# Block 0 of an attention kernel: output rows gathered in chunks of seven whole heads, the last four heads used where they are turned

## The chip, the cores and the metric

The kernel runs on one core of one Trainium2 chip. The metric is the device time of one execution in microseconds (us), lower is better. PE is the tensor engine, DVE the vector engine, ACT the scalar engine, POOL the GpSimd engine, and SP the engine whose queue issues most of the DMAs.

## The reference: what is computed

One transformer layer on 2048 rows of 576 values, in float32: attention with 32 query heads of 18 values that share one key and one value head, then a bilinear feed-forward network of width 4608, each behind a layer norm and with a residual.

```python
x = A_x
h = x + _A_ref(_layernorm(x, axis=-1), A_wq, A_wk, A_wv, A_wo)
h2 = h + _B_ref(_layernorm(h, axis=-1), B_w_gate, B_w_up, B_w_down)
# _A_ref: softmax(q k^T * 18**-0.5) v per head, the heads side by side (32*18 = 576), times wo
# _B_ref: ((x w_gate) * (x w_up)) w_down
```

## The kernel before, in words

The 2048 rows are cut into four blocks of 512 queries. Attention runs over block (b), group of four heads (g, eight of them), key tile (t, sixteen) and half of the group (two): each step is a **pair** (`pair`, L473), which multiplies keys and queries of two heads into PSUM (L493, PE) and takes the exponential of the 128x1024 result (L494, ACT). Some pairs later PE multiplies the exponentials with the values into `acc` (`values`, L498). One block is 256 pairs, the kernel has 1024; `n_pair` counts them. A product with float32 accuracy is made of three matmuls: each operand is split into a high part (a cast) and a low part (a subtraction), and high x high, low x high and high x low are added up (`split`, L85).

**Stages.** After keys and values, a loop (L985 to L995) runs pairs of block 0 together with the query projections of all blocks (`queries`, L311, matmuls at L329). One turn of this loop is a **round**: two pairs, some six steps of projection, one call of `run_aux`, and one step of `down_weights`. After 224 pairs comes `guard` (L380), a branch that is only taken for extreme scores. Block 0 goes on with `steps` (L873) up to pair 256, and then the first pairs of block 1 are put between the last pieces of block 0's output projection (`fill`, L864) until its residual rows are complete and normed. Then the feed-forward network runs block by block (`ffn`, L797), with the remaining pairs spread among its matmuls.

**The heads' way to the output projection.** When a group's sixteen key tiles are done, `flush` (L501) turns `acc` on DVE into `os` (L509), and puts `normalise` into the list `aux` for the round after the next. `normal_heads` (L531) divides by the row sums (L538 to L542) and turns once more (L545), into `ob[:, 4]`, or for group 7 into `ob[:, 0]`. There each head stands in its own 32 partitions: the row sum in the first, its 18 rows in the next. DMAs on SP (L552) bring the heads together, 18 rows after 18 rows, into chunks of 128 partitions: `ob[:, 0]` to `ob[:, 3]`. A head across a chunk's border needs two DMAs, and the last 64 rows (chunk 4) are written twice, to partitions 0 to 63 and 64 to 127, so that one matmul of 128 rows takes high and low part together: 40 DMAs for a block, 9 of them for group 7.

`normalise` (L523) then puts `chunk` (L555) into `aux`: chunk c after group 2c+1, chunk 4 also after group 7. For block 0 an entry becomes due three rounds after its `normalise` (L529). `chunk` splits the rows (a cast, L87 or for chunk 4 L96, and a subtraction, L88 or L97); in block 0 up to pair 256 the cast runs on DVE, then on ACT (L1009). It puts `project` (L601) into `aux`, which for block 0 may run from pair 236 on: for each of four row tiles and two halves 3 matmuls (2 for chunk 4) into a PSUM bank, of which three are in turn, and an addition to the residual on DVE (L617). After every second row tile `fill(2.4)` puts in two or three pairs. With chunk 4 the statistics of the norm follow on DVE. `run_aux` (L513) runs at most one due entry per call, the oldest first. Every engine works its queue in order, so the program's order is each engine's order.

**The weights of the second product.** Beside the query loop `down_weights` (L882) takes w_down apart, 18 pieces p = 0 to 17, in a fixed order by rounds: POOL loads a piece (L906), forms differences (L912) and casts (L920); DVE subtracts (L926); SP stores the result (L932). From p = 10 on it has three buffers, and a piece's steps come five rounds after the piece before's. The load of a piece stands on POOL right behind the casts of the piece before.

The loop of L985 with its list:

```python
self.pair(); ...; self.pair()
self.run_aux(1)
self.flush(len(self.pend) - 1)
next(work, None)        # one step of down_weights
```

Of the kernel before, what the change touches and what calls it, by code (L numbers as in the profile page):

```python
# [14 lines left out]
F32R = mybir.dt.float32r  # L18
# [6 lines left out]
P = 128  # L25
S, D, H, DH, F = 2048, 576, 32, 18, 4608
TB = 512
# [3 lines left out]
NG = H // 4  # L31
# [26 lines left out]
class Block:  # L58


    def __init__(self, tc, x, wq, wkv, wo, wgu, wd, cst, out):
        self.tc, self.nc = tc, tc.nc
        self.cast = tc.nc.scalar.copy
        self.x, self.wq, self.wkv, self.wo = x, wq, wkv, wo
        self.wgu, self.wd, self.cst, self.out = wgu, wd, cst, out
        self.pe, self.act, self.dve, self.sp = tc.nc.tensor, tc.nc.scalar, tc.nc.vector, tc.nc.sync

# [66 lines left out]
    def keys_values(self):  # L134
# [77 lines left out]
        def project(b):  # L212
            psk = psks[b] = (self.ps_f if b % 2 else self.ps_a)(f"psk{b}")
            for i, (w, m) in enumerate(passes(w_h, w_l, self.XT[b])):
                pe.matmul(psk, w, m, start=(i == 0), stop=(i == 13))
# [39 lines left out]
        stats(8, 12)  # L255
        scale(8, 12, pool)
        project(0)
        apply(1)
        stats(12, 13)
# [13 lines left out]
        q = self.qt[0, 0] = self.qp.tile([P, 2, TB], F32R, tag="q", name="q0_0")  # L273
        self.load_q(q, 0, 0)
        project(1)
        parts()
        late = keys(0)
        apply(3)
        twice(pool)
        late()  # L280
        turn(3)
        project(2)
        late = keys(1)
        parts()
# [238 lines left out]
    def normalise(self, b, g, os_):  # L523
        if g == 0:
            self.ob = self.op.tile([P, 5, TB], F32, tag="ob", name=f"ob{b}")
        self.normal_heads(b, g, os_)
        del self.os[g]
        for c in (g // 2,) * (g % 2) + (4,) * (b == 0 and g == NG - 1):
            self.aux.append((self.round + (2 if b == 0 else 0), lambda c=c: self.chunk(b, c), None))  # L529

    def normal_heads(self, b, g, os_):  # L531


        dve, ob = self.dve, self.ob
        o = os_.rearrange("p (k c) -> p k c", c=32)
        rc = self.op.tile([P, TB // 32], F32, tag="rc", bufs=2, name=f"rc{b}_{g}")
        if b == 0:
            dve.tensor_scalar(rc, o[:, :, 0], 1e-30, None, ALU.max)  # L538
            dve.reciprocal(rc, rc)
        else:  # L540
            dve.reciprocal(rc, o[:, :, 0])
        dve.tensor_tensor(o[:, :, 1:1 + DH], o[:, :, 1:1 + DH],  # L542
                          rc.unsqueeze(2).broadcast_to([P, TB // 32, DH]), ALU.mult)
        turned = ob[:, 4 if g < NG - 1 else 0]
        dve.transpose(turned, os_)  # L545
        for j in range(4):
            r, end = DH * (4 * g + j), DH * (4 * g + j + 1)
            p = 32 * j + 1
            while r < end:
                c, n = r // P, min(end, (r // P + 1) * P) - r  # L550
                for q in (r % P, 64 + r % P)[:1 if c < 4 else 2]:
                    self.sp.dma_start(ob[q:q + n, c], turned[p:p + n])  # L552
                r, p = r + n, p + n

    def chunk(self, b, c):  # L555

        if b == c == 0:
            self.oT = self.otp.tile([P, 9, TB], F32R, tag="oT", name=f"oT{b}")
        self.chunk_of(b, c)
        if b == 0:  # L560
            self.chunks.append(c)
        else:
            self.load_wo(c)
        self.aux.append((self.round, lambda: self.project(b, c),
                         lambda: b in self.h and (c in self.wos if b else self.n_pair >= self.wo_from)))

    def heads_to(self, b, c):
        if b == 0:
            return [self.oT[:, c], self.oT[:, 4 + c]] if c < 4 else [self.oT[:, 8]]
        return [self.o_hl[:, 0], self.o_hl[:, 1]] if c < 4 else [self.o_hl[:, 0]]  # L570

    def chunk_of(self, b, c):
        (self.split if c < 4 else self.split_tail)(*self.heads_to(b, c), self.ob[:, c])


    def load_wo(self, c):
# [11 lines left out]
    def load_wo_0(self):  # L588

        self.wo_0 = self.wp.tile([P, 2, 5, D], F32R, tag="X", bufs=1, name="wo_0")  # L590
        rs = [self.wp.tile([P, 2, D], F32, tag="wr", bufs=2, name=f"wo_r{i}") for i in range(2)]
        rs.append(self.wp.tile([P, 1, D], F32, tag="wor", bufs=1, name="wo_r2"))
        for i, r in enumerate(rs):
            self.sp.dma_start(r, self.wo[:, 2 * i:min(2 * i + 2, 5)])

        def parts():
            for c in range(5):
                self.split(self.wo_0[:, 0, c], self.wo_0[:, 1, c], rs[c // 2][:, c % 2], self.nc.gpsimd.tensor_copy)
        return parts

    def project(self, b, c):  # L601

        pe, dve = self.pe, self.dve
        h, to = self.h[b], self.heads_to(b, c)
        w = self.wos.pop(c) if b else self.wo_0[:, :, c]
        for s in range(NQ):
            sl = slice(s * P, (s + 1) * P)
            for n in range(2):
                y = self.ps_y(2 * s + n, f"yo{b}_{c}_{s}_{n}")
                d = slice(n * HD, (n + 1) * HD)  # L610
                if c < 4:
                    ms = [(to[0][:, sl], w[:, 0, d]), (to[1][:, sl], w[:, 0, d]), (to[0][:, sl], w[:, 1, d])]
                else:
                    ms = [(to[0][:, sl], w[:, 0, d]), (to[0][:, sl], w[:, 1, d])]
                for i, (m, k) in enumerate(ms):
                    pe.matmul(y[:, :HD], m, k, start=(i == 0), stop=(i == len(ms) - 1))  # L616
                dve.tensor_tensor(h[:, s, d], h[:, s, d], y[:, :HD], ALU.add)  # L617
            if b == 0:
                if c == 4:
                    self.statistics(b, s)  # L620
                if s % 2:
                    self.fill(2.4)
        if c == 3 and b:
            self.aux.append((self.round, lambda: self.chunk(b, 4), None))
        if c == 4:
            if b == 0:
                self.normed[b] = self.mv, self.rstd(self.mv[:, :, 1], f"b{b}")
            else:
                self.aux.append((self.round, lambda: self.all_statistics(b), None))
# [12 lines left out]
    def normal(self, b):  # L642
# [3 lines left out]
        for s in range(NQ):  # L646
            xh = self.p_tile([P, 640], f"xh2_{b}_{s}") if b else self.wp.tile([P, 640], F32, tag="wdo", bufs=WD_BUFS, name=f"xh2_0_{s}")
            self.dve.tensor_scalar(xh[:, 0:D], h[:, s, :], mv[:, s, 0:1], rs[:, s:s + 1], ALU.subtract, ALU.mult)
# [46 lines left out]
    def load_wd(self, n):  # L695

        while self.n_wd < n and self.n_wd < len(self.wd_list):
            b, p, j = self.wd_list[self.n_wd]
            w = self.wdo[b, p, j] = self.wp.tile([P, 2, HD], F32R, tag="wdo", bufs=WD_BUFS, name=f"wdo{b}_{p}_{j}")
            self.sp.dma_start(f32(w), self.wd_dram[p, :, j])  # L700
# [244 lines left out]
    def run(self):  # L945
# [12 lines left out]
        with ExitStack() as st:  # L958
# [38 lines left out]
            self.wp, self.hh, self.p2 = pool("w", 2), pool("hid", 4), pool("P2", 1)  # L997
            self.steps(lambda: self.n_pair < WO_FROM, work)
            wo_parts = self.load_wo_0()
# [11 lines left out]
            self.load_w(1)  # L1011
            self.load_wd(WD_BUFS - NQ)
            self.load_x(1)
# [18 lines left out]
            self.room()  # L1032
            self.load_wd(WD_BUFS)
            for b in range(NB):
# [8 lines left out]

ORDER = (0, 3, 4, 2, 5, 6, 1)
WD_BUFS = 10
WO_FROM = 208
STAGES = [(0, 0, P1, True, (0, 0), True), (1, 1, P1, True, (0, 0), True), (0, 2, P5, True, (1, 1), False),
          (0, 0, P6, False, (0, 1), True), (1, 1, P6, False, (0, 1), False), (0, 2, P3, False, (0, 1), False),
# [22 lines left out]
def f32(ap):  # L1071
    return ap.bitcast(F32)


def passes(W, Wl, XT):

    r = []
    for c in range(4):
        r += [(W[:, c], XT[:, c]), (W[:, c], XT[:, 4 + c]), (Wl[:, c], XT[:, c])]
    return r + [(W[:, 4], XT[:, 8]), (Wl[:, 4], XT[:, 8])]  # L1080


def drain(gen):
# [35 lines left out]
    return np.concatenate([a, t], axis=0).transpose(1, 0, 2)  # L1119


# [33 lines left out]
```

## Time and profile before

| | us |
|---|---|
| median of 3 runs (lowest to highest) | 2361.58 (2361.37 to 2367.57) |
| the profiled execution, its own time | 2361.63 |
| its span, first to last instruction | 2359.8 |
| from the first matmul behind the guard (L493) to the first turning of block 0's normed rows (L665) | 342.18 to 419.72 |

The profiled execution's own time is 1.83 us more than its span; that part lies around the first and last instruction. The page gives busy time by engine, and the trace lists the instructions of an engine in order of time with the idle time before each and what ended it. Where a row says x8, eight instructions of one kind are merged, and the time is that of all of them. An arrow in brackets names what the instruction had waited for.

### The profile page before, as it was taken

How to read it: one execution, taken by the hardware profiler on the slowest of the kernel's cores; microseconds unless marked ns; L12 is line 12 of the kernel's file. 1: busy time of each engine (PE TensorE's matmuls, PEld its weight loads, DVE VectorE, ACT ScalarE, POOL GpSimd, SP SyncE). 2: the span in 40 equal slices, each digit the busy share in tenths (PEclk: the TensorE clock that was granted, in tenths of full speed). 3: DMA queues.
4: the chain of work that ended last, by engine and by line, in shares of the span. 5: the costliest groups of instructions: out<-in, count | busy, mean ns of one | idle time of the engine just before them, and what ended most of it. 6: DMA issues, size and time to landing. Idle time of an engine off the chain costs nothing.

```text
span 2359.8 us, 46074 instructions
## 1 busy us (share of the span) xinstructions
PE 2291.4 (97%) x18217; PEld 1604.3 (68%) x18217; DVE 1165.5 (49%) x2062; ACT 1433.4 (61%) x1869; POOL 647.8 (27%) x803
## 2 busy tenths in 40 slices
PE   5999988999999999999999999999999999999999
PEld 4333324577777767777767667766777778888888
DVE  7546543444444444544444445444444476565565
ACT  4888766676777676667676776567676623232332
POOL 3545400121222222222221222312222223343333
PEclk9999999999999999999999999999999999999999
DMA  4686852443434333543333333443334335655543
GB/s 141 212 266 216 297 171 84 129 124 105 125 121 127 122 118 120 179 127 121 110 121 107 119 127 122 145 159 121 117 117 123 111 129 182 196 190 184 175 167 126
DMA packets 158090, 345.47 MB, mean 146 GB/s; under 512 B 16204, under 2 KB 48460, under 8 KB 157868
## 3 DMA queue, kind: packets, MB, share of 16 engines
q1 hardware_dynamic: 155276, 331.84, 43.7%
q0 software_dynamic: 2592, 10.62, 1.6%
q8 instruction: 146, 2.39, 0.4%
q14 instruction: 76, 0.62, 0.1%
HBM read 272.63 MB, written 55.67 MB: 139 GB/s over the span
## 4 chain that ended last, share of the span: by engine, by line
PE 80%; DVE 2%; issue 1%; ACT 1%; DMA 1%; POOL 1%; SPq 0%; DVEq 0%; ACTq 0%; POOLq 0%
PE y L777 16%; PE pg L817 15%; PE acc L498 15%; PE gu L817 12%; PE pu L817 9%; PE s L493 9%; PE yo L616 2%; PE y L735 1%; ACT P L494 0%; POOL h L785 0%; PE ye L735 0%; PE tx L665 0%; SPq L552 0%; DMA out_dram<-h 0%; DMA X<-X 0%
## 5 line engine op out<-in xcount | busy, mean ns | idle before, releaser
L494 ACT ACTIVATE P<-s 128x1024 f32<-128x1024 f32 x1024 | 1025.9, 1027 | 325.7 <-PE s L493 237.2
L817 PE MATMUL pg<-X,ws 64*128 64x512 f32 x2565 | 699.4, 391 | 0.0
L817 PE MATMUL pu<-X,ws 64*128 64x512 f32 x2565 | 699.3, 391 | 0.0
L785 POOL TENSOR_TENSOR h<-h,tmp 128x288 f32<-128x288 f32 x408 | 318.8, 811 | 877.8 <-ACT tmp L784 876.5
L817 PEld LDWEIGHTS pg<-X,ws 64*128 64x128 f32 x2565 | 476.4, 186 | 60.0 <-DMA wdo<-wd_dram 0.8
L817 PEld LDWEIGHTS pu<-X,ws 64*128 64x128 f32 x2565 | 473.5, 186 | 34.7
L498 PE MATMUL acc<-P,V 128*32 128x512 f32 x4096 | 491.8, 600 | 3.3 <-DVE os L509 2.6
L493 PE MATMUL s<-q,kT 56*128 56x512 f32 x2048 | 440.7, 425 | 9.9 <-DVEq L383 6.1
L777 PEld LDWEIGHTS y<-wdo,room 128*128 128x128 f32 x2856 | 387.8, 189 | 52.3 <-issue 43.3
L777 PE MATMUL y<-wdo,room 128*128 128x288 f32 x2856 | 405.0, 300 | 5.2 <-DVE h L780 5.1
L784 ACT COPY tmp<-y 128x288 f32<-128x288 f32 x408 | 162.8, 399 | 331.3 <-PE y L777 324.7
L780 DVE TENSOR_TENSOR h<-h,y 128x288 f32<-128x288 f32 x544 | 234.5, 453 | 244.3 <-PE y L777 241.5
L493 PEld LDWEIGHTS s<-q,kT 56*128 56x128 f32 x2048 | 196.0, 186 | 213.9 <-ACT P L494 117.0
L817 PE MATMUL gu<-X,ws 64*128 64x512 f32 x2646 | 308.2, 389 | 0.3 <-DMA X<-X 0.2
L87 POOL CAST ws<-wr 128x1152 fp32r<-128x1152 f32 x144 | 167.9, 1166 | 446.0 <-PE pu L817 176.6
L817 PEld LDWEIGHTS gu<-X,ws 64*128 64x128 f32 x2646 | 255.1, 184 | 46.9 <-issue 4.1
L498 PEld LDWEIGHTS acc<-P,V 128*32 128x32 f32 x4096 | 114.6, 109 | 252.2 <-issue 232.2
L88 DVE TENSOR_TENSOR ws<-wr,ws 128x1152 fp32r<-128x1152 f32 x144 | 194.6, 1351 | 79.3 <-POOL ws L87 79.3
L839 DVE TENSOR_TENSOR hf<-pu,g 128x512 f32<-128x512 f32 x95 | 65.7, 691 | 332.2 <-ACT g L835 332.2
L88 DVE TENSOR_TENSOR room<-S,room 128x1024 fp32r<-128x1024 f32 x68 | 83.3, 1225 | 157.4 <-ACT room L87 157.4
L835 ACT COPY g<-gu 128x512 f32<-128x512 f32 x49 | 28.9, 590 | 134.6 <-PE gu L817 134.6
L87 ACT CAST room<-hf 128x256 fp32r<-128x256 f32 (+1 forms) x144 | 73.9, 513 | 47.2 <-DVE hf L839 47.0
(165 smaller groups left out, 1561.2 us busy)
## 6 DMA issues: line engine op xcount, KB each, us to landing
wdo<-wd_dram SPq DMA_DIRECT2D x492, 288.0 KB
wr<-in_wgu_dram SPq DMA_DIRECT2D x144, 576.0 KB
wd_dram<-wd_room SPq DMA_DIRECT2D x20, 1008.0 KB
q<-q_dram SPq DMA_DIRECT2D x64, 216.0 KB
q_dram<-qs SPq DMA_DIRECT2D x16, 504.0 KB
X<-X SPq DMA_DIRECT2D x28, 256.0 KB
wd_dram<-wd_hi SPq DMA_DIRECT2D x7, 1008.0 KB
wd_dram<-wd_src SPq DMA_DIRECT2D x7, 1008.0 KB
```

The lines of the kernel that those rows point to most:

```text
L87: (copy or self.cast)(hi, src)
L88: self.dve.tensor_tensor(lo, src, f32(hi), ALU.subtract)
L493: self.pe.matmul(s_[:, i], self.kT[o:o + 56, t * P:(t + 1) * P], q[o:o + 56, pr], start=True, stop=True)
L494: self.act.activation(p_, s_, AF.Exp, scale=SCALE)
L498: self.pe.matmul(acc[32 * j:32 * j + 32, :], self.V[:, t, :], Ps[j // 2][:, j % 2, :], start=(t == 0), stop=(t == NT - 1), skip_group_chec ...
L616: pe.matmul(y[:, :HD], m, k, start=(i == 0), stop=(i == len(ms) - 1))
L777: pe.matmul(y[:, :HD], m[:, t * P:(t + 1) * P], k, start=(first and j == 0), stop=(j == 2), skip_group_check=True)
L780: dve.tensor_tensor(hs, hs, y[:, :HD], ALU.add)
L784: act.copy(z, y[:, :HD])
L785: pool.tensor_tensor(hs, hs, z, ALU.add)
L817: pe.matmul(ps, w[o:o + 64, wk, c], X[o:o + 64, xk, c], start=(j == 0), stop=(j == 26))
L839: dve.tensor_tensor(hf, pu, g, ALU.mult)
```

## The change

For block 0 alone, chunks 0 to 3 become seven whole heads each (126 rows), so no head is cut, and each head takes one DMA. The last four heads (group 7) are not gathered: their turned tile in `ob[:, 4]` is chunk 4 as it stands, 32 partitions a head, and a second layout of wo, `wo0`, has zero rows where that tile holds row sums and nothing. Chunk 4 is therefore split like the others and takes three matmuls for each output instead of two. Chunk 3 is complete after group 6 instead of 7. Chunks 0 to 3 become due seven rounds after their `normalise` instead of three, chunk 4 one round after. Blocks 1 to 3 are as before. The diff, without the passing on of the new argument; line 1 of the new file is an added empty line:

```diff
@@ normalise
-        for c in (g // 2,) * (g % 2) + (4,) * (b == 0 and g == NG - 1):
-            self.aux.append((self.round + (2 if b == 0 else 0), lambda c=c: self.chunk(b, c), None))
+        c = ({1: 0, 3: 1, 5: 2, 6: 3, 7: 4} if b == 0 else {1: 0, 3: 1, 5: 2, 7: 3}).get(g)
+        if c is not None:
+            self.aux.append((self.round + (LANDING if b == 0 and c < 4 else 0), lambda: self.chunk(b, c), None))
@@ normal_heads
-        turned = ob[:, 4 if g < NG - 1 else 0]
+        turned = ob[:, 4 if b == 0 or g < NG - 1 else 0]
         dve.transpose(turned, os_)
+        if b == 0 and g == NG - 1:
+            return
         for j in range(4):
-            r, end = DH * (4 * g + j), DH * (4 * g + j + 1)
+            r, end, m = DH * (4 * g + j), DH * (4 * g + j + 1), rows(b, 0)
             p = 32 * j + 1
             while r < end:
-                c, n = r // P, min(end, (r // P + 1) * P) - r
-                for q in (r % P, 64 + r % P)[:1 if c < 4 else 2]:
+                c, n = r // m, min(end, (r // m + 1) * m) - r
+                for q in (r % m, 64 + r % m)[:1 if c < 4 else 2]:
@@ chunk, heads_to, chunk_of
-            self.oT = self.otp.tile([P, 9, TB], F32R, tag="oT", name=f"oT{b}")
+            self.oT = self.otp.tile([P, 8, TB], F32R, tag="oT", name=f"oT{b}")
-            return [self.oT[:, c], self.oT[:, 4 + c]] if c < 4 else [self.oT[:, 8]]
+            n = rows(b, c)
+            return [self.oT[0:n, c % 4], self.oT[0:n, 4 + c % 4]]
-        (self.split if c < 4 else self.split_tail)(*self.heads_to(b, c), self.ob[:, c])
+        to = self.heads_to(b, c)
+        (self.split_tail if b and c == 4 else self.split)(*to, self.ob[0:rows(b, c), c])
@@ load_wo_0, project
-            self.sp.dma_start(r, self.wo[:, 2 * i:min(2 * i + 2, 5)])
+            self.sp.dma_start(r, self.wo0[:, 2 * i:min(2 * i + 2, 5)])
-        w = self.wos.pop(c) if b else self.wo_0[:, :, c]
+        w = self.wos.pop(c) if b else self.wo_0[0:rows(b, c), :, c]
-                if c < 4:
+                if c < 4 or b == 0:
@@
+LANDING = 6
+def rows(b, c):
+    return 7 * DH if b == 0 and c < 4 else P
+def _by_sevens(w):
+    a = np.zeros((5, P, w.shape[1]), w.dtype)
+    a[:4, :7 * DH] = w[:28 * DH].reshape(4, 7 * DH, -1)
+    a[4].reshape(4, 32, -1)[:, 1:1 + DH] = w[28 * DH:].reshape(4, DH, -1)
+    return a.transpose(1, 0, 2)
```

More of the change, by code (lines that the diff above doesn't have):

```diff
@@ L58, with __init__ @@
 class Block:
-    def __init__(self, tc, x, wq, wkv, wo, wgu, wd, cst, out):
+    def __init__(self, tc, x, wq, wkv, wo, wo0, wgu, wd, cst, out):
         self.tc, self.nc = tc, tc.nc
         self.cast = tc.nc.scalar.copy
-        self.x, self.wq, self.wkv, self.wo = x, wq, wkv, wo
+        self.x, self.wq, self.wkv, self.wo, self.wo0 = x, wq, wkv, wo, wo0
         self.wgu, self.wd, self.cst, self.out = wgu, wd, cst, out
@@ L1138 @@
         "wo": _tail_twice(i["A_wo"]),
+        "wo0": _by_sevens(np.asarray(i["A_wo"])),
         "wgu": wgu,
```

## The prediction

> **What bounds the kernel now.** I read the page first: the span, the busy times and the 40 slices. Then the waits of PE and of DVE up to the feed-forward network, then the order of time around each long one, and last POOL's rows.
>
> ```profile
> span 2359.8 us, 46074 instructions
> PE 2291.4 (97%) x18217; PEld 1604.3 (68%) x18217; DVE 1165.5 (49%) x2062; ACT 1433.4 (61%) x1869; POOL 647.8 (27%) x803
> PE   5999988999999999999999999999999999999999
> PE yo L616 <- DVE h L617: 5.2, 1, 5.2
> DVE oT L87 <- DMA ob<-ob: 16.9, 3, 8.4
> DVE wd_room L926 <- POOL wd_room L920: 7.7, 1, 7.7
> ```
>
> PE is busy 97% of the span; what it idles lies mostly in the start and in slices 6 and 7 (59 us each), so before the feed-forward network. The columns of the wait rows are the total, the count and the longest. Two single waits of PE stand out, 5.2 us for a DVE addition and the one shown next, 6.2 us for a DVE copy, and DVE itself waits three times, 16.9 us in all, for the DMAs that gather heads. The last row, DVE waiting 7.7 us for POOL, hurts nobody in this profile; I come back to it.
>
> The first wait of PE, in order of time, with PE's work and clock in windows (PE busy, its instructions, then PEld, DVE, ACT, POOL, granted clock, DMA share, GB/s):
>
> ```profile
> 233.52 0.50 DVE L87 CAST oT<-ob 128x512 fp32r<-128x512 f32 x1 [8.42 <-DMA ob<-ob]
> 235.14 3.61 DVE L926 TENSOR_TENSOR wd_src<-wd_src,wd_hi 128x864 f32<-128x864 f32 x2
> 238.67 0.68 DVE L336 COPY qs<-psr 126x512 f32<-126x512 f32 x1
> 239.41 0.70 PE L329 MATMUL psq<-XT,wq_h 64*72 64x512 f32 x1 [6.21 <-DVE qs L336]
> 225.00:230.00 5.00, 5.00 (x40) 2.04 (x37) 0.10 (x1) 4.19 (x6) 0.00 (x0) 1.00 0.70 216
> 239.00:242.00 3.00, 2.56 (x8) 0.80 (x12) 2.90 (x6) 0.64 (x1) 1.33 (x2) 0.50 1.04 348
> 242.00:244.00 2.00, 2.00 (x12) 0.64 (x6) 2.00 (x2) 0.43 (x2) 0.00 (x0) 0.50 1.03 344
> 244.00:246.00 2.00, 2.00 (x12) 0.76 (x12) 0.10 (x1) 1.32 (x2) 0.00 (x0) 0.50 1.02 302
> ```
>
> Chunk 1's cast stands on DVE for 8.42 us until its rows have landed. Behind it are its subtraction, two pieces of L926 and then L336, which empties a PSUM bank that PE needs. PE idles 6.21 us and then runs at half clock: 32 matmuls in the 6.6 us from 239.41 to 246, where the undisturbed window does 8 a microsecond, 4.0 us. So this stall costs 6.2 + 2.6 = 8.8 us.
>
> The second, at the end of block 0:
>
> ```profile
> 388.69 6.71 SPq L552 DMA_DIRECT2D ob<-ob  x9
> 397.06 0.62 ACT L96 CAST oT<-ob 128x512 fp32r<-128x512 f32 x1 [4.53 <-DMA q<-m_dram]
> 397.71 0.69 DVE L97 TENSOR_TENSOR oT<-ob,oT 64x512 fp32r<-64x512 f32 x1 [5.38 <-ACT oT L96]
> 398.94 1.09 PE L616 MATMUL yo<-wo,oT 128*128 128x288 f32 x3 [5.23 <-DVE h L617]
> 401.11 2.71 PE L616 MATMUL yo<-wo,oT 128*128 128x288 f32 x12
> 374.28 1.88 PE L616 MATMUL yo<-wo,oT 128*128 128x288 f32 x12
> 419.72 2.53 PE L665 MATMUL tx<-C,xh 128*128 128x128 f32 x20 [1.23 <-ACT P L494]
> ```
>
> Nine DMAs of group 7 take SP 6.71 us to issue, 0.75 us each. Chunk 4's cast waits for them on ACT (the row names the last DMA queue event; the nine are what L96 reads), its subtraction waits on DVE, and chunk 3's additions, which free the banks of PE, are queued behind that. PE idles 5.23 us and again comes back at half clock: twelve matmuls in 2.71 us against 1.88 us.
>
> **The change, part by part.**
>
> *The count of pairs.* I followed `n_pair`, the rounds and `aux` by the code. Before: group 7's `normalise` at 259 pairs, chunk 3 at 262, chunk 4 at 263, projections at 264 and 269, feed-forward from 280. After: chunk 3 at 256 and its projection at 258, `normalise` of group 7 at 264, chunk 4 at 265, its projection at 266, feed-forward again from 280. So nothing moves behind 420 us, and the gain can only come from before.
>
> *The end of block 0.* The 5.23 us of idle PE go, since chunk 4 has no DMA any more. The half clock goes too: 2.71 - 1.88 = 0.83 us of the twelve, 1.09 - 3 x 0.157 = 0.62 us of the three (0.157 is 1.88/12), and about 0.5 us of four scores at 399.95 (1.22 us) against 0.74 us elsewhere:
>
> ```profile
> 399.95 1.22 PE L493 MATMUL s<-q,kT 56*128 56x512 f32 x4
> 379.53 0.74 PE L493 MATMUL s<-q,kT 56*128 56x512 f32 x4
> 390.99 0.62 ACT L87 CAST oT<-ob 128x512 fp32r<-128x512 f32 x1 [0.47 <-issue]
> 391.64 0.69 DVE L88 TENSOR_TENSOR oT<-ob,oT 128x512 fp32r<-128x512 f32 x1 [2.98 <-ACT oT L87]
> ```
>
> Together 1.9 us. Added are eight matmuls, 8 x 0.157 = 1.25 us, all on PE's path. What is late next is chunk 4's own chain: the adds of chunk 3, `normalise`, cast and subtraction, then the first product. The last two take 0.62 + 0.69 us and some 0.1 us between, and PE has one more pair to work on. The bounds are 0, as chunk 3's rows above had it before, and the bare 1.4 us; with chunk 4's cast also queued behind the exponentials on ACT I take 1.0. If DVE is late there, the cast holds up ACT, and so the exponentials behind it and PE. Sum: 5.2 + 1.9 - 1.25 - 1.0 = **4.9 us gained**; bounds 3 and 7.5, as pairs that fill the gap now are then paced by ACT instead of PE or not.
>
> *Chunks 0 to 2 four rounds later.* A round takes 2.37 us (the exponentials of the rows below start 226.44 and 228.81), so the split comes 9.5 us later. Chunk 1 would reach DVE about 240, its last DMA landed by 233.5: no wait. The other 8.5 of DVE's 16.9 us are those of chunks 0 and 2; behind chunk 0's PE waited 0.43 us (the row at 154.27), which I count as 0.4 gained, behind chunk 2's not at all.
>
> ```profile
> 226.44 1.96 ACT L494 ACTIVATE P<-s 128x1024 f32<-128x1024 f32 x2 [0.40 <-PE s L493]
> 228.81 1.02 ACT L494 ACTIVATE P<-s 128x1024 f32<-128x1024 f32 x1 [0.40 <-PE s L493]
> 154.27 0.49 PE L329 MATMUL psq<-XT,wq_h 64*126 64x512 f32 x1 [0.43 <-DVE qs L336]
> 222.90 0.58 POOL L906 DMA_DIRECT2D wd_room<-in_wd_dram  x1
> 232.08 3.79 POOL L912 TENSOR_TENSOR wd_room<-wd_room 128x288 f32<-128x288 f32 x4 [8.60 <-DMA wd_room<-in_wd_dram]
> 235.81 3.94 POOL L920 CAST wd_room<-wd_room 128x864 fp32r<-128x864 f32 x2
> 241.31 0.57 POOL L906 DMA_DIRECT2D wd_room<-in_wd_dram  x1 [1.55 <-DVE qs L339]
> 251.31 3.19 POOL L912 TENSOR_TENSOR wd_room<-wd_room 128x288 f32<-128x288 f32 x4 [9.43 <-DMA wd_room<-in_wd_dram]
> 254.45 1.99 POOL L920 CAST wd_room<-wd_room 128x864 fp32r<-128x864 f32 x2
> 260.54 4.21 POOL L912 TENSOR_TENSOR wd_src<-wd_src 128x288 f32<-128x288 f32 x4 [3.58 <-DMA wd_src<-in_wd_dram]
> 260.41 0.72 DVE L509 STREAM_TRANSPOSE os<-acc 128x512 f32<-128x512 f32 x1 [1.40 <-PE acc L498]
> 293.10 2.00 POOL L920 CAST wd_room<-wd_room 128x864 fp32r<-128x864 f32 x2
> 294.04 1.96 DVE L926 TENSOR_TENSOR wd_room<-wd_room 128x864 f32<-128x864 f32 x1 [7.70 <-POOL wd_room L920]
> 295.93 0.68 DVE L336 COPY qs<-psr 126x512 f32<-126x512 f32 x1
> 296.66 0.50 PE L329 MATMUL psq<-XT,wq_h 64*126 64x512 f32 x1 [0.81 <-DVE qs L336]
> ```
>
> *What then comes due: POOL.* These rows decide the forecast. POOL's work for w_down is one chain: load, wait, differences, cast, next load. From the load of piece 12 at 222.90 to the cast of piece 16 at 293.10 there is almost no slack in it but the 1.55 us at 241.31; five pieces take 72 us, 14.4 us each. The program gives a piece five rounds, 5 x 2.37 = 11.9 us. So POOL falls behind by 2.5 us a piece, and PE's stall at 233 hid this: at 294.04 DVE has waited 7.70 us for piece 16, the next thing on DVE is L336, and PE waits 0.81 us for it. PE thus stands level with POOL at 296.66, after losing 8.8 us at 233. Without that loss it gets there up to 8.8 us sooner and waits. Partly it waits before: DVE's part of piece 13 comes just ahead of group 4's turning (L509, now 260.41, then due at 260.4 - 8.8 = 251.6), but piece 13's first half is cast about 255.4, so L509 comes about 256.4 and PE, which wants `acc` again one round after 251.6, stands some 3 us. The rest, 4 to 5 us, it stands at L336 ahead of 296.
>
> So the phase gains only what the chain itself gains. The load of piece 13 waits for a buffer whose store stands on SP behind the gathering DMAs; there is one of these less (five become four), 0.75 us, so I take 1.0. Bounds: -2 (busier DMAs make a load later) and +4 (1.55 us for the wait, 1.95 us if L920 at 235.81 takes 1.99 us instead of 3.94 us, 0.4 us from chunk 0). Against it stands the clock: after a stall of 4 to 5 us PE comes back at half clock, which cost 1.9 and 2.6 us above; bounds 0 and 2.6, I take 2.0. With chunk 0's 0.4 us, which lies ahead of the chain, the phase comes to 1.0 - 2.0 + 0.4 = **-0.6 us**.
>
> The Trainium skill, "TensorE: Matmul & The Clock Gate", Part 1, says that PE is throttled to half after about one idle window of 3.4 us, and the window runs free of the program. In this trace the clock is 0.50 from 239 to 246 after 6.2 us of idling, which agrees. By that rule a stall of 3 us may keep the clock and one of 5 us won't, so it speaks for the 2.0 and against a gain that comes back as waits. The same skill, "SBUF — State Buffer", section "SBUF: two separate sides", has it that a two-input DVE operation and a POOL operation that reads block each other for the whole instruction; the rows 3.61 us (L926) and 3.94 us (L920), which overlap, fit it. By that rule the chain would shorten by 1.95 us and the sum would be 1 us better.
>
> *Edits at nothing.* Rows 126 instead of 128 in the splits and matmuls, the other layout of wo (as many bytes, loaded and cast behind the guard's wait), the smaller `oT`, 12 DMAs fewer on SP: PE and DVE work by columns here, and SP waits anyway. If that cover is gone, a DMA is 0.75 us of SP. Group 7's turning into `ob[:, 4]` waits for group 6's DMAs, a whole group older. The query load behind the nine DMAs on SP goes out earlier; nobody waits for it.
>
> Sum: 4.9 - 0.6 = 4.3 us from the execution's own time of 2361.63 us (span 2359.8 us and 1.83 us around it), which is within 0.1 us of the median: **2357.3 us**.
>
> **The rivals.**
>
> A, the forecast: the end's stall goes, POOL takes back the other; 2357.3, own range 2354 to 2360. For it: the 0.81 us at 296.66. Chance 0.53.
>
> B, POOL's chain moves up with PE. For it: POOL waited 3.58 us for one load of the chain and 8.60 and 9.43 us for others, so waits for the DMAs, more than POOL's work, make its length, and the DMAs' share was 1.02 to 1.04 just after PE's stall. Then 8.8 + 0.4 + 4.9 = 14.1 us: 2347.5. Chance 0.25.
>
> C, the gain at the end doesn't come either: chunk 4's chain and ACT's pace take the place of the DMA wait, as 22 exponentials of 1.02 us and the products leave PE little to run ahead. Then 0 to 2 us: 2360.5. Chance 0.15.
>
> D, slower: the rounds from 233 to 296 come closer together, their query traffic falls into the loads, and two loads are waited for 9.4 instead of 3.6 us. Piece 16 is then 11.6 us late; less 4.9 and 0.4 us at the other places, plus 2 us of half clock, the kernel is 8.3 us slower, 2370. It decides from piece 16's L926 later than about 299, where it eats the end's gain. Against it: in the undisturbed window at 225 the DMAs' share is 0.70. Chance 0.07.
>
> **How the numbers follow.** About 0.3%, 7.1 us, is what a measurement of this kernel can tell from no change. Faster by more (under 2354.5) are B and some 0.08 of A: 0.33. Slower by more is D: 0.07. The rest, 0.60, is within. The range takes in A, C and nearly all of B and leaves D out: 2347 to 2362.
>
> **What would show it.** Right: no wait of DVE for the gathering DMAs, no PE stall near 233, DVE waiting for POOL at pieces 13 and 16 with PE waits of 3 to 5 us behind L509 and L336, piece 16's L926 about 293; the turning at L665 some 4.3 us sooner than 419.72. Wrong: piece 16 well before 290 (B) or after 299 (D), a new wait of PE ahead of chunk 4's first product of more than 2 us (C), or a different count of pairs ahead of the feed-forward network.

## The result and the profile after

The changed kernel takes 2358.82 us (median of 22 runs, 2354.22 to 2364.05), the kernel before 2362.84 us (median of 22 runs beside them, 2355.52 to 2369.16): 4.0 us less. The ratio is 0.9983, with a 95% interval of 0.9975 to 0.9991, so the change is small but real, and the forecast of 4.3 us less met it. The two profiled executions lie only 0.6 us apart (2361.63 and 2361.02); why, the runs show below.

From the page of the changed kernel (its lines are up to six higher than those of the kernel before: L616 is now L622, L926 is L932):

```profile
span 2359.3 us, 46065 instructions
PE 2293.9 (97%) x18225; PEld 1607.0 (68%) x18225; DVE 1167.9 (50%) x2063; ACT 1432.3 (61%) x1868; POOL 647.4 (27%) x803
```

PE has its eight matmuls more, and nothing else of note changed in the totals. The waits of PE and of DVE up to the feed-forward network (total, count, longest) tell more:

```profile
PE acc L499 <- DVE os L510: 5.1, 3, 3.7
PE psq L330 <- DVE qs L337: 4.5, 1, 4.5
PE yo L622 <- DVE h L623: 0.6, 1, 0.6
DVE wd_room L932 <- POOL wd_room L926: 12.5, 3, 9.2
```

DVE's 16.9 us behind the gathering DMAs are gone without a rest, and so are the 5.2 us of PE at block 0's end. But DVE's waits for POOL rose from 7.7 to 12.5 us, and PE still stands 4.5 us behind L337. In order of time, POOL's pieces 12, 13 and 16 and what hangs on them:

```profile
228.63 2.83 POOL L926 CAST wd_room<-wd_room 128x864 fp32r<-128x864 f32 x2
240.67 0.58 POOL L912 DMA_DIRECT2D wd_room<-in_wd_dram  x1 [9.21 <-DMA wd_dram<-wd_room]
250.84 3.98 POOL L918 TENSOR_TENSOR wd_room<-wd_room 128x288 f32<-128x288 f32 x4 [9.60 <-DMA wd_room<-in_wd_dram]
292.00 1.99 POOL L926 CAST wd_room<-wd_room 128x864 fp32r<-128x864 f32 x2
292.94 1.96 DVE L932 TENSOR_TENSOR wd_room<-wd_room 128x864 f32<-128x864 f32 x1 [9.18 <-POOL wd_room L926]
295.55 0.64 PE L330 MATMUL psq<-XT,wq_h 64*126 64x512 f32 x1 [4.45 <-DVE qs L337]
288.00:290.00 2.00, 2.00 (x18) 0.64 (x14) 0.00 (x0) 1.60 (x2) 1.05 (x2) 1.00 1.08 384
296.00:298.00 2.00, 1.91 (x10) 0.98 (x13) 1.93 (x5) 0.00 (x0) 0.03 (x1) 0.50 0.59 240
298.00:300.00 2.00, 2.00 (x10) 0.34 (x8) 1.43 (x3) 1.02 (x1) 2.00 (x1) 0.50 0.82 253
300.00:302.00 2.00, 2.00 (x10) 1.20 (x10) 1.86 (x5) 1.02 (x1) 0.29 (x1) 0.50 0.98 342
```

The matmul that stood at 296.66 us before stands at 295.55 us: 1.1 us gained. The windows (PE's busy time with its instructions second, granted clock third from the end) show the price: six microseconds at half clock, in which PE does 30 instructions instead of 54, so 2.7 us lost. The first row is new: POOL had cast piece 12 by 231.5 us, and then waited 9.21 us for a store.

The end of block 0 in the changed kernel:

```profile
389.05 1.91 PE L622 MATMUL yo<-wo,oT 126*128 126x288 f32 x12
399.76 0.61 ACT L88 CAST oT<-ob 128x512 fp32r<-128x512 f32 x1
400.52 0.37 PE L622 MATMUL yo<-wo,oT 128*128 128x288 f32 x1 [0.54 <-ACT oT L88]
401.15 1.75 PE L622 MATMUL yo<-wo,oT 128*128 128x288 f32 x11 [0.27 <-DVE oT L89]
405.58 0.66 PE L622 MATMUL yo<-wo,oT 128*128 128x288 f32 x3 [0.59 <-DVE h L623]
344.23 1.31 PE L494 MATMUL s<-q,kT 56*128 56x512 f32 x4 [6.96 <-SPq L384]
418.14 2.40 PE L671 MATMUL tx<-C,xh 128*128 128x128 f32 x20 [0.94 <-ACT P L495]
```

Chunk 4's first product waits 0.54 + 0.27 us for its cast and subtraction, and its last three matmuls wait 0.59 us for an addition: 1.40 us in all are left of the stall. From the guard (344.23) to the turning of the normed rows (418.14) it is 73.9 us; before, 77.5.

### The profile page after: what moved, and what is told of

It is laid out like the page before. It is cut to its first block, busy times and chain, and to the rows that moved or that the text cites. A ratio compares the mean times of both kernels' runs of the same rounds, so it can differ in the third digit from the quotient of the medians.

```text
span 2359.3 us, 46065 instructions
## 1 busy us (share of the span) xinstructions
PE 2293.9 (97%) x18225; PEld 1607.0 (68%) x18225; DVE 1167.9 (50%) x2063; ACT 1432.3 (61%) x1868; POOL 647.4 (27%) x803
## 4 chain that ended last, share of the span: by engine, by line
PE 80%; DVE 2%; issue 1%; ACT 1%; POOL 1%; DMA 0%; SPq 0%; DVEq 0%; ACTq 0%; POOLq 0%
PE y L783 16%; PE acc L499 15%; PE pg L823 15%; PE gu L823 12%; PE pu L823 10%; PE s L494 9%; PE yo L622 2%; ACT P L495 1%; PE y L741 0%; POOL h L791 0%; PE ye L741 0%; PE tx L671 0%; DMA X<-X 0%; DVE h L623 0%; DVE h L786 0%
## 5 line engine op out<-in xcount | busy, mean ns | idle before, releaser
L89 DVE TENSOR_TENSOR ws<-wr,ws 128x1152 fp32r<-128x1152 f32 x144 | 194.7, 1352 | 79.2 <-POOL ws L88 76.3
L88 ACT CAST room<-hf 128x256 fp32r<-128x256 f32 (+1 forms) x144 | 73.9, 513 | 48.3 <-DVE hf L845 48.1
```

The source lines that it names most:

```text
L88: (copy or self.cast)(hi, src)
L89: self.dve.tensor_tensor(lo, src, f32(hi), ALU.subtract)
```

## The experiments

**Theory P**: the gain is block 0's end alone; the later splits save a stall near 233 us, but POOL's chain of w_down pieces hands it back at 250 to 297 us. **Rival Q**: the chain follows PE. The first four kernels split the change and the chain's pace. The stretches are collected in a table after them.

**e1, the later splits alone.** The kernel before with

```diff
-  self.aux.append((self.round + (2 if b == 0 else 0), lambda c=c: self.chunk(b, c), None))
+  self.aux.append((self.round + (0 if b else 6 if c < 3 else 2), lambda c=c: self.chunk(b, c), None))
```

> The kernel before with one edit: chunks 0 to 2 of block 0 become due seven rounds after their normalise instead of three; gathering, chunk 3 and chunk 4 are as before. Theory P (POOL's chain of w_down pieces sets the pace from piece 12 to 16, so what the later chunks save near 233 us comes back as PE waits behind L509 and L336 before 296 us, with a half clock after it): between 1 us faster and 2 us slower than before; no long PE wait near 233 us, PE waits of 2 to 5 us near 253 and 291 us, the first projection matmul after the last of them (at 296.66 us before) at 295 to 297 us. Rival Q (the chain follows PE): 7 to 9 us faster, that matmul at 288 us or sooner. The end of block 0, from the guard's first matmul to the turning of the normed rows, stays 77 to 78 us in both.

Measured: 2361.98 us against 2361.81 us, ratio 1.0006 (0.9994 to 1.0019). PE's waits of this kernel and the longest of them:

```profile
PE acc L498 <- DVE os L509: 8.7, 4, 4.0
262.38 1.94 PE L498 MATMUL acc<-P,V 128*32 128x512 f32 x8 [3.96 <-DVE os L509]
```

The wait near 233 us is gone and one of 3.96 us at 262 us is there, behind piece 13 as the prediction had it, with half clock after it (eight matmuls in 1.94 us instead of 1.06). The second wait, expected near 291 us, did not come (0.35 us at 300.59). In its place the wait near 142 us, ahead of all this, took 3.79 us in this execution instead of 2.01; e8 and e9 come back to it. The time is the same. Q is out: a stall of 8.8 us was removed for nothing.

**e2, the gathering and group 7 in place alone.** The changed kernel with `LANDING = 2`.

> The changed kernel with LANDING 2 instead of 6: whole-head chunks and group 7 in place stay, chunks 0 to 3 are due three rounds after their normalise as before. Theory P: the whole gain of the change is at block 0's end, so 3.5 to 6 us faster than before; DVE waits again some 8 us for the gathering DMAs near 225 to 233 us and PE 6 us behind it; from the guard's first matmul to the turning of the normed rows 73 to 75 us instead of 77.5. Rival R (the gain needs the later splits): within 1 us of before.

Measured: 2356.40 us against 2361.81 us, ratio 0.9981 (0.9972 to 0.9990), 5.4 us less by the medians and 4.5 by the ratio.

```profile
DVE oT L88 <- DMA ob<-ob: 15.3, 3, 8.3
239.37 0.46 PE L330 MATMUL psq<-XT,wq_h 64*72 64x512 f32 x1 [3.19 <-DVE qs L337]
```

DVE's waits for the gathering DMAs are all back in the query loop, and the gain stands. Together with e1, which gains nothing, this puts the whole effect of the change at block 0's end, as far as the times can tell. PE's part of the stall was 3.2 us in this execution, not 6.

**e3, the chain given its time.** The changed kernel with pieces of w_down six rounds apart throughout:

```diff
-            return 6 * min(p, 10) + 5 * max(p - 10, 0)
+            return 6 * p
```

> The changed kernel with one more edit: pieces of w_down from 10 on come six rounds apart instead of five (begin is 6 * p for all), so POOL gets 14.2 us a piece instead of 11.9. Theory P: DVE no longer waits for POOL at pieces 13 and 16 by more than 2 us, PE's waits behind L509 and L336 near 257 and 291 us go, the half clock after them too: 5 to 9 us faster than the changed kernel, 9 to 13 us faster than before. Rival S (the DMAs' share near 1.0 sets the pace, not the program's rounds): the loads come later as well, the waits move on, and it is within 1.5 us of the changed kernel.

Measured: 2354.01 us against 2361.81 us, ratio 0.9969 (0.9957 to 0.9982): 7.3 us faster than before by the ratio, some 3 us faster than the changed kernel. PE's waits behind L510 and L337, over the whole stretch:

```profile
PE acc L499 <- DVE os L510: 3.6, 2, 2.0
```

No wait is longer than 2.0 us, and L337 isn't among them any more. The direction was right, the size below the 9 to 13 us expected. The interval overlaps the changed kernel's (0.9975 to 0.9991), so the 3 us between the two are likely, not settled.

**e4, the same pace in the kernel before.** The same edit there.

> The kernel before with begin 6 * p alone. Theory P: the stall near 233 us stays (it is the gathering DMAs'), only the 0.8 us at 296 us goes: between 2 us faster and 1 us slower than before, so that the six rounds are worth much less here than in the changed kernel. Rival T (the five-round pitch costs the kernel by itself, whatever the chunks do): as much faster as in the changed kernel, 5 us or more.

Measured: 2361.92 us against 2361.81 us, ratio 0.9996 (0.9987 to 1.0005). T is out: the pace is worth nothing without the change. One thing was not as expected: PE's stall near 233 us was short, and another came behind L509.

```profile
240.18 0.57 POOL L906 DMA_DIRECT2D wd_room<-in_wd_dram  x1 [11.07 <-DMA wd_dram<-wd_room]
237.12 0.45 PE L329 MATMUL psq<-XT,wq_h 64*72 64x512 f32 x1 [0.97 <-DVE qs L336]
297.23 1.45 PE L498 MATMUL acc<-P,V 128*32 128x512 f32 x8 [3.17 <-DVE os L509]
```

**What pins the chain.** In every profile so far the load of piece 13 went out between 240.2 and 244.5 us, whatever POOL had done before; in e4 POOL waited 11.07 us for it (the row above). The load needs the buffer of piece 10, and the store of piece 10 stands on SP behind the query load and the gathering DMAs of group 3. **Theory P2**: that store pins the chain. **Rival S**: the full DMAs do. So e5 moves this one store:

```diff
-  for d, f in ((6, lambda p=p: store(p)), (-3, ...), ..., (5, lambda p=p: low(p, 1))):
+  for d, f in ((-3, ...), ..., (5, lambda p=p: low(p, 1)), (5 if p == 10 else 6, lambda p=p: store(p))):
```

> The changed kernel with one edit: the store of piece 10 stands one round earlier on SP, so ahead of the query load and the gathering DMAs of group 3 instead of behind them. Theory P2 (what pins POOL's chain is the load of piece 13, which in all six profiles so far goes out at 240 to 244.5 us because it waits for piece 10's store; the pieces behind it follow): the load of piece 13 goes out at 237 us or sooner, POOL's wait before it falls under 3 us, DVE's wait for POOL ahead of piece 16 and PE's wait behind L337 near 291 us fall by 3 us or more, and the kernel is 3 to 7 us faster than the changed one, 7 to 11 us faster than before. Rival S (the DMAs are full from 236 to 254 us anyhow): the load goes out earlier and lands at the same 250 us; within 1.5 us of the changed kernel.

Measured: 2351.57 us against 2361.49 us, ratio 0.9960 (0.9946 to 0.9974): 9.4 us faster than before, 5.4 us faster than the changed kernel by the ratios. SP, POOL, DVE and PE of this kernel, and its DMA share in the contested stretch:

```profile
221.73 0.52 SPq L938 DMA_DIRECT2D wd_dram<-wd_room  x1
231.99 0.57 POOL L912 DMA_DIRECT2D wd_room<-in_wd_dram  x1
237.02 5.08 POOL L918 TENSOR_TENSOR wd_room<-wd_room 128x288 f32<-128x288 f32 x4 [4.46 <-DMA wd_room<-in_wd_dram]
287.46 1.96 DVE L932 TENSOR_TENSOR wd_room<-wd_room 128x864 f32<-128x864 f32 x1 [7.86 <-POOL wd_room L926]
290.08 0.49 PE L330 MATMUL psq<-XT,wq_h 64*126 64x512 f32 x1 [0.98 <-DVE qs L337]
236.00:254.00 18.00, 18.00 (x138) 6.78 (x135) 11.63 (x14) 15.65 (x17) 8.59 (x7) 1.00 0.99 318
```

The load goes out at 231.99 us, without a wait, and is waited for 4.46 us instead of 9.60; piece 16 is ready 5.5 us sooner (287.46 against 292.94), PE waits 0.98 us instead of 4.45, and no half clock follows. DVE's wait for POOL ahead of piece 16 fell less than expected, from 9.18 to 7.86 us, as DVE too got there sooner. The DMAs were nearly as full in this stretch as in the changed kernel (0.99 against 1.03) and the load still landed at 237 us, not at 250, so S is out. By the times it is closer: the intervals of this kernel (up to 0.9974) and of the changed one (from 0.9975) just clear each other. The moved store was tried only on top of the change; what it is worth in the kernel before is open.

**e6, both.** Six rounds and the earlier store.

> The changed kernel with six rounds a piece and the store of piece 10 one round earlier. P2: with six rounds POOL's chain already has its time, so the earlier store adds 0 to 3 us to it: 7 to 11 us faster than before. Rival S: the same as six rounds alone, about 7 us faster than before.

Measured: 2352.85 us against 2361.49 us, ratio 0.9966 (0.9954 to 0.9978). No better than e5 alone, and not told apart from e3 (0.9957 to 0.9982). In none of the three profiles is a wait of PE from 250 us to the end of the query loop longer than 1.6 us, so either edit frees the chain.

**e7, the later splits once the chain is free.** Six rounds with `LANDING = 2`.

> The changed kernel with six rounds a piece and chunks 0 to 3 due three rounds after their normalise, as before the change. Theory P: with POOL's pace relieved the later splits are worth something for the first time, so this is 1 to 6 us slower than six rounds with the later splits (about 2 to 6 us faster than before), with DVE waiting again for the gathering DMAs and PE behind it. Rival U (the later splits never matter): within 1 us of the changed kernel with six rounds.

Measured: 2357.60 us against 2361.49 us, ratio 0.9982 (0.9971 to 0.9993).

```profile
DVE oT L88 <- DMA ob<-ob: 15.2, 3, 7.0
PE psq L330 <- DVE qs L337: 5.0, 1, 5.0
```

The wait for the gathering DMAs is back with 5.0 us of PE, and the kernel is 3 us slower than e3 by the ratios. The two intervals overlap a little (0.9971 to 0.9982), so this is likely rather than settled: the later splits pay once POOL's chain is out of the way.

**e8 and e9, both kernels once more**, for the 0.6 us between the first two profiles.

> The kernel before once more, unchanged, for a second profile of it. The wait of PE for L509 near 141 us was 2.0 us in the first profile, and 3.3 to 3.8 us with a half clock after it in most profiles of the other kernels, the changed one among them. If that is chance between executions, it comes in some executions of this kernel too: 2.0 to 3.8 us here. If the change causes it, it is 2.0 us here again. From the guard's first matmul to the turning of the normed rows: 77 to 79.5 us.

> The changed kernel once more, unchanged. The load of piece 13 goes out at 239 to 245 us behind a wait for piece 10's store, DVE waits for POOL ahead of piece 16, and PE behind L337 or L510 by 3 us or more somewhere between 250 and 297 us, with a half clock after it; from the guard's first matmul to the turning of the normed rows 73 to 74.5 us. The wait for L510 near 143 us is 2.0 to 3.8 us if it is chance between executions.

Measured, one execution each: 2359.23 us and 2362.17 us. The waits at group 1's turning, the kernel before first, then the changed one:

```profile
141.46 1.93 PE L498 MATMUL acc<-P,V 128*32 128x512 f32 x8 [2.00 <-DVE os L509]
239.30 0.70 PE L329 MATMUL psq<-XT,wq_h 64*72 64x512 f32 x1 [5.11 <-DVE qs L336]
```

```profile
144.87 1.93 PE L499 MATMUL acc<-P,V 128*32 128x512 f32 x8 [3.57 <-DVE os L510]
242.17 0.57 POOL L912 DMA_DIRECT2D wd_room<-in_wd_dram  x1 [9.71 <-DVE wd_room L932]
297.78 0.79 PE L330 MATMUL psq<-XT,wq_h 64*126 64x512 f32 x1 [5.34 <-DVE qs L337]
```

In the changed kernel's first profile this wait was:

```profile
143.89 1.94 PE L499 MATMUL acc<-P,V 128*32 128x512 f32 x8 [3.72 <-DVE os L510]
```

and in the first profile of before it was 2.01 us, with full clock after it. So the changed kernel's first execution lost 1.7 us and a half clock there, and it was 1.4 us late before that wait began (140.17 against 138.79 us). Together this hides the 4 us in the pair. Near 142 us PE waits 2.0 to 3.8 us in all profiles, kernels with and without the change: 3.8 in e1 and 3.6 in e4, which gather as before, 2.0 in e3 and 2.1 in e10, which are changed. So this wait isn't the change's. A single execution of each kernel can't show a difference of 4 us; here the changed one happens to be slower. The late load (242.17) and the wait behind L337 (5.34 us) come again. The row of the load names DVE's L932 as the last event, so this profile doesn't itself show that it was piece 10's store.

**e10, the eight matmuls by themselves.** The changed kernel with `if c < 4:` again in `project`, which leaves out the low part of the last four heads.

> The changed kernel with two products instead of three for block 0's chunk 4: the low part of the last four heads times wo is left out, so the result is less exact. It measures the eight added matmuls by themselves: if they lie on PE's path at 0.157 us each, the stretch from the guard's first matmul to the turning of the normed rows is 1.0 to 1.5 us shorter than in the changed kernel (72.3 to 73 us against 73.4 to 74.1); if they lie beside ACT's exponentials, it is within 0.4 us of it.

Measured: 2351.56 us in one execution; from the guard to the turning 73.0 us:

```profile
336.17 1.31 PE L494 MATMUL s<-q,kT 56*128 56x512 f32 x4 [6.57 <-SPq L384]
372.58 1.88 PE L622 MATMUL yo<-wo,oT 126*128 126x288 f32 x12
409.14 2.40 PE L671 MATMUL tx<-C,xh 128*128 128x128 f32 x20 [0.94 <-ACT P L495]
```

That is 0.9 us less than the 73.9 of the changed kernel, inside the range expected, but profiles of kernels with all three products run from 72.8 to 74.1 us in this stretch. A shorter stretch settles it. It begins at the last twelve matmuls of chunk 2's projection, which come ahead of everything in which the two kernels differ; in the changed kernel and the kernel before these are

```profile
380.69 1.88 PE L622 MATMUL yo<-wo,oT 126*128 126x288 f32 x12
```

```profile
377.73 1.87 PE L616 MATMUL yo<-wo,oT 128*128 128x288 f32 x12
```

From there to the turning it is 409.14 - 372.58 = 36.56 us here, against 37.45 and 37.41 us in the changed kernel's two profiles and 37.41 to 37.44 in e3, e5 and e6. So the eight matmuls cost 0.87 us net, less than the 1.25 us of the sum and than the 1.0 to 1.5 us expected, and more than nothing.

Up to chunk 4's projection e10 is the changed kernel, so its profile is a third one of the query loop. It looks different from the other two:

```profile
238.04 0.57 POOL L912 DMA_DIRECT2D wd_room<-in_wd_dram  x1 [7.21 <-DMA wd_dram<-wd_room]
256.28 1.75 PE L499 MATMUL acc<-P,V 128*32 128x512 f32 x8 [2.61 <-DVE os L510]
287.65 1.97 DVE L932 TENSOR_TENSOR wd_room<-wd_room 128x864 f32<-128x864 f32 x1 [5.74 <-POOL wd_room L926]
```

The load of piece 13 waits for the store as before, though it goes out 2.6 to 4.1 us sooner. PE waits 2.61 us behind piece 13 and not at all behind L337, and piece 16 comes 5.3 to 7.5 us sooner.

The stretches, from the trace of each, in us:

| kernel | psx (L374 or L375), end of the query loop | guard to turning | chunk 2's last twelve matmuls to turning |
|---|---|---|---|
| before; again | 330.45; 327.81 | 77.5; 77.7 | 41.99; 42.19 |
| e1 later splits; e4 before, six rounds | 330.01; 328.12 | 79.2; 79.3 | 42.84; 42.81 |
| changed; again | 331.67; 333.58 | 73.9; 73.9 | 37.45; 37.41 |
| e10 two products | 324.01 | 73.0 | 36.56 |
| e2 in place alone; e7 six rounds, LANDING 2 | 327.71; 330.34 | 73.4; 72.8 | 36.97; 36.95 |
| e3 six rounds; e5 store 10; e6 both | 320.93; 323.84; 319.36 | 74.1; 73.9; 73.2 | 37.43; 37.41; 37.44 |

The column from the guard on has two levels and no overlap: 78.4 us on average for four profiles with the old end, 73.6 us for the seven with the new one and all its products. But it holds the half clock behind the guard's wait, which lasted 6 to 7 us in four executions (before twice, e6, e7) and 9 to 10 us in the others, whatever the kernel. The last column leaves that out: 42.0 to 42.8 us with the old end, 37.4 us with the new one (37.0 us in e2 and e7, where chunk 3 is due earlier). So the end gains 4.5 to 5.4 us, 5.0 on average.

The psx column warns against reading one profile: the same code reached psx at 331.67, 333.58 and 324.01 us. So the early ends of e3, e5 and e6 don't by themselves show what their edits are worth; that rests on the times.

## Why the prediction was right, step by step

- **Block 0's end, 4.9 us gained.** Right: 5.0 us on average, and e1 and e2 show that this alone is the change's gain. Two terms of the sum were off and cancel: the matmuls cost 0.87 us instead of 1.25 (e10), and PE's waits in chunk 4's projection, its own chain and the late addition, come to 1.40 us instead of 1.0. That the sum came out so close is partly luck. One cost was not in it: from psx to the guard's first matmul it is 11.7 to 12.1 us in the four profiles with the old end and 12.1 to 12.6 in the eight with the new one, about 0.5 us more; the runs don't show why.
- **The count of pairs.** The order came as counted: chunk 3's projection ahead of group 7's `normalise`, chunk 4's after it, and the gain stays ahead of the feed-forward network, whose first matmul moves by 1.7 us (427.08 to 425.37) in the profiled pair, with the query loop's scatter in it. For the same reason the turning at L665 was no usable sign: it was to come 4.3 us sooner, and came 1.6 us sooner in the first pair (418.14) and 2.3 us later in the second (419.60 against 417.27).
- **POOL takes back the stall at 233.** Right by the times: e1 gains nothing, and e5 gains once the chain is freed (e3 likely). The numbers of the first profile: L330 1.1 us sooner (1.0 taken), the wait there 4.45 us (4 to 5), piece 16's L932 at 292.94 (about 293), the half clock 2.7 us (2.0 taken). The other wait, put at 3 us behind piece 13, was 0.75 us in this execution, 0.87 in e9, 2.61 in e10 and 3.96 in e1. Where the time is handed back, and how much of it, so differs from execution to execution; in e10 PE didn't wait behind L337 at all.
- **Why the chain is late: wrong for its start.** The prediction read POOL as a chain without slack that falls behind by 2.5 us a piece. Ahead of piece 13 the changed kernel's profile contradicts it: POOL cast piece 12 at 228.63 instead of 235.81 us, 7 us ahead, and stood 9.21 us for a store that SP issues behind other DMAs. Behind that load the picture holds: no load waits to go out any more, and four pieces take 53.3 us (240.67 to 293.99), 13.3 us each, more than the five rounds' 11.9. The 1.55 us wait of the profile before was the visible end of that pin (in e8 POOL came to this load too late to wait), and was counted as a small term of the bounds. e5 puts it in the right place. The clue was there: of the loads of pieces 12 to 16 this was the one that POOL could not issue at once.
- **Rival B** (the chain follows, 14.1 us) failed on the cause given, since the loads follow the pinned store; with the store freed, e5 gains 9.4 us, of which some 5 are the end's, so about half of the 9.2 us that B gave to this phase. In e10 piece 16 came at 287.65 us, on B's side of the sign, with the load held up all the same. **Rival C** failed, as the end's gain came in full. **Rival D** failed: piece 13's differences began 0.5 us sooner in the first pair (250.84 against 251.31) and 3.1 us later in the second (252.44 against 249.36), and piece 16 stayed under D's 299 us (292.94 and 295.16).
- **Chunk 0's 0.4 us** can't be seen: the wait near 142 us, just ahead of it, varies by 1.8 us.

The rule of the Trainium skill, "TensorE: Matmul & The Clock Gate", Part 1, that PE is throttled after an idle window of about 3.4 us, agrees with the half clock after 4.45 us here, but not with the half clock after 2.00 us in e8, below. The rule of "SBUF — State Buffer", section "SBUF: two separate sides", that two-input DVE operations and reading POOL operations block each other, would have made the chain 1.95 us shorter; the cast took 2.83 us instead of 3.94 us, again beside a DVE subtraction (3.98 us), but the store held the next load, so it gave no time.

## What to carry to other kernels

A stall that is removed gives time only up to the next thing that arrives at a fixed time, so look for what another engine delivers just after it: here a wait of 0.8 us, 57 us later, told that PE and POOL stood level. For a chain of loads, compute and stores, ask of each load what buffer it needs and where the store that frees it stands in its queue; one store moved by one round was worth 5.4 us by the ratios, about as much as the whole change. A gain of 0.2% needs many runs and stretches compared over several profiles, not one pair of them.

## What the runs showed of the hardware that was not expected

The half clock did not need a long stall. In e8 PE waited 2.00 us at 141.46 and came back at half clock (eight matmuls in 1.93 us); in the first profile of the same kernel it waited 2.01 us at 140.80 and came back at full clock (1.06 us). At the same place waits of 2.0 to 2.1 us in e3, e6 and e10 came back at half clock too (eight matmuls in 1.94 us in each). The windows of PE around the first:

```profile
138.00:139.40 1.40, 1.40 (x12) 0.37 (x4) 1.33 (x3) 1.01 (x2) 0.43 (x1) 1.00 1.07 372
139.40:141.40 2.00, 0.05 (x2) 0.00 (x0) 1.97 (x4) 1.83 (x2) 0.00 (x0) 0.99 0.60 200
141.40:143.00 1.60, 1.54 (x8) 0.20 (x8) 1.46 (x5) 0.00 (x0) 0.22 (x1) 0.50 0.86 281
143.00:145.00 2.00, 2.00 (x12) 1.36 (x10) 2.00 (x3) 0.50 (x1) 0.36 (x1) 0.55 0.74 206
```

The same wait can so cost 2 us or some 4 us (an estimate: about 3.4 us at half clock lose 1.7 us); what decides it the runs don't show. That may be part of the several microseconds by which executions of one kernel differ; it wasn't tried by itself.
